# Regrouping the helper copies of the first attention unit, and two rewritten instruction orders, in a block-sparse attention and GELU kernel

## The chip, the cores and the metric

The kernel runs on one core of one Trainium2 chip. The metric is the device time of one execution in microseconds (us), lower is better; it is the time of the single core that is used. A core has TensorE (PE, with weight loads shown apart as PEld), VectorE (DVE), ScalarE (ACT), GpSimd (POOL) and SyncE (SP), each of which works through its own instructions in order, and 16 DMA engines that all queues share.

## The reference

Inputs are q, k and v, each 4 batches x 8 heads x 768 tokens x 64, three sampled block numbers for each of 24 query blocks, and two weight matrices. Attention is block-sparse: a token sees the block of 32 keys that it is in, its two neighbours, the first and the last block, and the sampled blocks; queries of the first and the last block see everything.

```
scores = q @ k^T / 8
mask   = |blk_i - blk_j| <= 1, or blk_i or blk_j is 0 or 23, or blk_j in sampled_blocks[blk_i]
attn   = softmax(where(mask, scores, -1e9))
x      = (attn @ v) as 3072 tokens x 512
out    = gelu_exact(x @ w_in) @ w_out          # w_in 512x2048, w_out 2048x512
```

## The kernel before

Each batch is split in two units, so there are eight. A unit of the first kind (0, 2, 4, 6) holds the query blocks 1 to 11 in three groups of up to four blocks, and the two dense blocks 0 and 23, whose queries see all keys. A unit of the second kind holds the blocks 12 to 22. For each unit the kernel does attention, then the first matrix product with GELU (FFN1, `ffn1_step`), then the second product (FFN2, `ffn2_pieces`), whose 48 matmuls of 128x512 are spread as filler through the attention of the next unit. Unit 0 has no FFN2 before it, so its filler is 32 products whose result nobody reads (`idle_products`); of these, the numbers in the tuple `small` are 32 columns wide and the others 512.

The order of work within an attention is written out by hand, as a string of words that `attention` reads from left to right. A round is one set of scores: in unit 0, rounds 0 to 3 are the dense ones, 4 and 5 are group a, 6 and 7 group b, 8 and 9 group c. For round i, `si` issues the score matmuls (L364), `mi` the row maxima on DVE (L390, L393), `ei` the exponentials on ACT (L407, L411) and `ti` the transposition of the result on DVE (L424, L429). For group g, `wg` multiplies by the values (PE, L489; dense L450), `dg` divides (DVE, L504 to L509) and `og` transposes on PE (L521) and copies to the FFN1's input on ACT (L529; dense L534). `fN` issues N filler products, `G` loads ACT's table for GELU, `S` stores finished outputs, and `x..` runs one of the named extras. Since every engine is in order, a word's place in the string sets what its instructions wait behind. The score banks in PSUM are three, so a score round waits until the exponentials of an earlier round have freed one.

Sampled keys and values are at block numbers known only at run time, so they are gathered into the tile `gb`, one copy for each sampled block (`gather_pairs`, L319): 128x128 for keys, 128x264 for values. In unit 0, DVE copies the keys of group a, POOL those of groups b and c; the values go to `kn` (group a) and `g` (groups b and c), all by POOL but for the three copies of the last block of group c, which ACT makes (extra `xv`). The keys that do not depend on the sampling are called fixed: the neighbours (L295, in three parts called lanes) and the first and last block (L306 by SP's transfers, or L308). DVE makes them for group a (`xj`, `xi`, `xh`), ACT the neighbours for group b (`xf0`, `xf1`) and group c (`xf2`), and SP transfers the first and last block of both groups, six transfers in all.

Four quarters of w_in are asked for on POOL's queue, each between two stretches of gather copies (L161). `later_loads` (`xl`) makes POOL wait for the latest divided tile (L172), then asks for w_out and for the keys and queries of batch 1. After unit 0, DVE copies all its keys into the tile `kv` that unit 1 reads (L789).

Of the kernel before, what the change touches and what calls it, by code (L numbers as in the profile page):

```python
# [20 lines left out]
def kernel(  # L21
# [147 lines left out]

    def hold_loads(x):  # L170

        nc.gpsimd.tensor_copy(mark, x)  # L172
# [108 lines left out]
    def gather_fixed(kT, place, copy=None, part=None, lanes=range(3)):  # L281
# [5 lines left out]
        for run in runs if part != 1 else ():  # L287
            i0 = place[run[0]]
            assert i0 % 3 == 0
            for lane in range(min(3, len(run))):  # L290
                if lane not in lanes:
                    continue
                m, g0 = len(range(lane, len(run), 3)), i0 // 3
                c0, j = BW + KC * lane, run[0] + lane - 1
                copy(  # L295
                    groups[:, g0:g0 + m, c0:c0 + 3 * BW].rearrange("p g (w c) -> p g w c", c=BW)[:, :, :, 0:KC],
                    kT[:, j:j + 3 * m, :].rearrange("p (g w) c -> p g w c", w=3))
# [4 lines left out]
        for to, n0 in ((groups[:, at, 0:3 * KC].rearrange("p g (l c) -> p g l c", c=KC), 0),  # L302
                       (groups[:, at, 4 * BW:GW].rearrange("p g (l x) -> p g l x", x=DW)[:, :, :, NR * BW:DW], NB - 1)):
            if copy is nc.sync:
                for x in range(n):
                    nc.sync.dma_start(out=to[:, x], in_=kT[:, n0:n0 + 1, :].to_broadcast([P, 3, KC]))  # L306
            else:
                copy(to, kT[:, None, n0:n0 + 1, :].to_broadcast([P, n, 3, KC]))  # L308
# [388 lines left out]
    last = block_numbers(grps[2][-1:], ACT)  # L697
# [6 lines left out]
    def fixed(t, *how):  # L704
        gather_fixed(k0, {j: units[0].place[j] for j in grps[t]}, *how)
    fixed(1, nc.sync, 1)
    fixed(2, nc.sync, 1)
# [3 lines left out]
    others |= block_numbers(grps[0], POOL)  # L711
    load_w_in(1)
    gather(units[0], grps[2], others, 0, KC, nc.gpsimd)

    def values_of(t):

        def ask():
            js = grps[t] if t != 2 else grps[t][:-1]
# [25 lines left out]
    attention(units[0], idle_products(32, (30, 31)),  # L744
# [7 lines left out]
               "f2": lambda: fixed(2, nc.scalar.copy, 0), "v0": values_of(0), "v1": values_of(1),  # L752
               "v2": values_of(2), "v": lambda: gather(units[0], grps[2][-1:], last, KC, BW, nc.scalar), "m": more_numbers(J1[3:5]), "n": more_numbers(J1[5:8]),
# [4 lines left out]
    def next_keys(b):  # L758
# [24 lines left out]
    for n, unit in enumerate(units):  # L783
# [3 lines left out]
        if nxt is not None and not fresh:  # L787
            if n == 0:
                nc.vector.tensor_copy(kvs[0][:, :, 0:KC], k0)  # L789
# [79 lines left out]
```

## Time and profile before

| | us |
|---|---|
| median of three runs | 270.31 (269.55 to 270.35) |
| the profiled execution | 270.44 |
| span within it, which the views show | 268.7 |
| PE busy | 248.3 (92% of the span) |
| DVE, ACT, POOL busy | 202.1, 206.8, 110.1 |

Times in the views count from the start of the span. A row of the timeline gives start, duration, engine, source line, operation, output <- inputs with their shapes, and how many instructions stand together; in brackets stands how long the engine was idle before, and what ended that. "issue" is idle time in which the engine waited for nothing that the profile shows. A row of the windows view gives a stretch from:to, its length, then the busy time of PE, PEld, DVE, ACT and POOL with the number of instructions, the granted TensorE clock (1.00 is full speed), the DMA share and GB/s. The first unit's attention lies between about 10 and 37.6, its FFN1 up to 47.5, and the second unit's attention from there to 70.5.

### The profile page before, as it was taken

What the parts mean: (1) busy time and instruction counts of PE and PEld (TensorE: products, weight loads), DVE (VectorE), ACT (ScalarE), POOL (GpSimd) and SP (SyncE); (2) the same over time, 40 slices, a digit from 0 to 9 for tenths busy, and PEclk for the clock granted to TensorE, in tenths of its full rate; (3) what the DMA queues carried; (4) which work ended last, traced back from release to release, by engine and by line L of the source; (5) the groups of instructions that cost most, each with busy time, mean ns of one, the idle gap of its engine ahead of it and who ended that gap; (6) DMA issues with size and microseconds to landing.
All of it is one profiled execution on the core that took longest, in us unless ns stands there. A gap on an engine that the chain in (4) does not pass through costs nothing.

```text
span 268.7 us, 11541 instructions
## 1 busy us (share of the span) xinstructions
PE 248.3 (92%) x4909; PEld 143.5 (53%) x4944; DVE 202.1 (75%) x472; ACT 206.8 (77%) x382; POOL 110.1 (41%) x216
## 2 busy tenths in 40 slices
PE   1799879989999999999999999999999999999994
PEld 1634566455564566545555566455645655465544
DVE  7599878788998987699988986696979891981000
ACT  8789856978869867897879956987799676995611
POOL 7798987854964001934970005900040340000000
PEclk9999999999999999999999999999999999999999
DMA  6999779999999117913995119911101110111012
GB/s 97 186 185 187 110 101 191 205 129 132 99 164 134 44 43 158 118 40 62 136 141 143 43 46 145 91 43 44 40 2 41 44 41 0 41 44 44 0 39 82
DMA packets 76007, 24.42 MB, mean 91 GB/s; under 512 B 65585, under 2 KB 73010, under 8 KB 75954
## 3 DMA queue, kind: packets, MB, share of 16 engines
q0 software_dynamic: 57536, 13.64, 54.6%
q1 hardware_dynamic: 18418, 10.03, 14.5%
q8 instruction: 39, 0.64, 1.0%
q14 instruction: 14, 0.11, 0.1%
HBM read 27.26 MB, written 6.29 MB: 125 GB/s over the span
## 4 chain that ended last, share of the span: by engine, by line
PE 78%; ACT 7%; DVE 5%; issue 4%; DMA 3%; POOL 1%; ACTq 0%; POOLq 0%
PE hp L544 31%; PE op L587 23%; PE av L489 7%; PE sc L364 7%; ACT pp L407 3%; DMA qn<-in_q_dram 3%; PE tx L521 2%; PE op L619 2%; PE pt L241 2%; PE av L450 2%; DVE pT L424 1%; DVE nm L390 1%; PE av L619 1%; ACT pp L411 1%; DVE xh L509 1%
## 5 line engine op out<-in xcount | busy, mean ns | idle before, releaser
L544 PE MATMUL hp<-xT,w_in_sb 128*128 128x384 bf16 (+2 forms) x536 | 84.9, 319 | 0.0
L587 PE MATMUL op<-w_out_sb,g 128*128 128x512 bf16 x302 | 75.5, 380 | 3.5 <-issue 2.5
L407 ACT ACTIVATE pp<-sc,nm 128x256 bf16<-128x256 f32 x176 | 74.0, 543 | 3.7 <-DVE nm L390 3.1
L544 PEld LDWEIGHTS <-w_in_sb 128*128 128x128 bf16 x536 | 51.1, 98 | 32.8
L390 DVE TENSOR_REDUCE nm<-sc 128x4 f32<-128x1024 f32 (+1 forms) x48 | 52.9, 1116 | 12.8 <-PE sc L364 12.8
L566 ACT ACTIVATE g<-hp 128x768 bf16<-128x768 f32 x56 | 45.0, 809 | 22.7 <-PE hp L544 22.6
L587 PEld LDWEIGHTS <-g 128*128 128x128 bf16 x336 | 29.1, 98 | 34.3 <-issue 7.0
L319 DVE COPY gb<-kv 128x392 bf16 x177 | 35.9, 279 | 0.0
L424 DVE STREAM_TRANSPOSE pT<-pp 128x512 f32<-128x512 f32 (+1 forms) x48 | 30.7, 651 | 3.4 <-ACT pp L407 3.4
L319 POOL COPY gb<-kv 128x392 bf16 x54 | 26.4, 535 | 13.7 <-PE av L489 13.4
L172 POOL COPY mark<-gb 1x1 bf16<-1x1 bf16 x6 | 1.1, 179 | 70.9 <-DVE gb L319 70.9
L489 PEld LDWEIGHTS <-pT 64*32 64x32 bf16 (+1 forms) x2400 | 25.2, 91 | 8.9 <-issue 3.9
L489 PE MATMUL av<-kv,pT 64*32 64x130 bf16 (+1 forms) x1344 | 27.5, 221 | 2.4 <-issue 1.8
L529 ACT COPY xT<-tx 128x512 bf16<-128x512 bf16 (+3 forms) x32 | 13.6, 451 | 14.8 <-PE tx L521 14.8
L148 POOL DMA_DIRECT2D kv<-in_v_dram x32 | 23.0, 726 | 2.4 <-issue 2.3
L364 PE MATMUL sc<-gb,qT 64*32 64x256 bf16 x704 | 17.9, 273 | 2.0 <-issue 0.9
L435 ACT ACT_TABLE_LOAD x15 | 19.2, 1283 | 0.3
L509 DVE TENSOR_TENSOR xh<-av,rec 128x512 bf16<-128x512 f32 (+2 forms) x28 | 18.2, 651 | 1.0
L364 PEld LDWEIGHTS <-qT 64*32 64x32 bf16 x832 | 9.9, 90 | 17.1 <-issue 9.0
L393 DVE TENSOR_REDUCE nm<-sc 128x1 f32<-128x768 f32 x16 | 14.8, 943 | 4.5 <-PE sc L364 4.5
L411 ACT ACTIVATE pp<-sc,nm 128x768 bf16<-128x768 f32 x16 | 17.2, 1109 | 1.1 <-DVE nm L393 1.1
L571 ACT COPY os<-op 128x512 f32<-128x512 f32 (+1 forms) x23 | 13.2, 574 | 5.8 <-PE op L619 4.3
(85 smaller groups left out, 257.9 us busy)
## 6 DMA issues: line engine op xcount, KB each, us to landing
out_dram<-os SPq DMA_DIRECT2D x23, 256.0 KB, 2.1
kv<-in_v_dram POOLq DMA_DIRECT2D x32, 96.0 KB, 3.7
w_in_sb<-in_moe_w_in_dram POOLq DMA_DIRECT2D x4, 512.0 KB, 7.8
w_out_sb<-in_moe_w_out_dram POOLq DMA_DIRECT2D x8, 256.0 KB, 8.0
kn<-in_k_dram POOLq DMA_DIRECT2D x4, 384.0 KB, 8.0
qn<-in_q_dram POOLq DMA_DIRECT2D x4, 384.0 KB, 9.1
qn<-in_q_dram POOLq DMA_DIRECT2D x12, 128.0 KB, 5.4
kn<-in_k_dram POOLq DMA_DIRECT2D x12, 128.0 KB, 6.0
```

Of the source, the lines that this page charges most:

```text
L148: nc.gpsimd.dma_start(out=kvs[b % 2][32 * hh:32 * hh + 32, 0:NB, c0:c0 + D], in_=v[b, h].rearrange("(n p) d -> p n d", p=BL))
L319: copy(to[:, None, :], src[:, bass.ds(at[j][r], 1), :])
L364: nc.tensor.matmul(o, lhsT=qT[rows, j // 4, pr, BL * (j % 4):BL * (j % 4) + BL], rhs=rhs(rows, pr), start=True, stop=True)
L390: nc.vector.tensor_reduce(out=nm[:, 0:2 * n].rearrange("p (g j) -> p g j", g=2), in_=A4[:, :, 0:n, :], op=ALU.max, axis=AX.X, negate=True)
L407: nc.scalar.activation(at[:, x // n, x % n], A[:, a:a + 256].rearrange("p (e c k) -> p e c k", e=2, k=BL), AF.Exp, bias=nm[:, x:x + 1])
L411: nc.scalar.activation(pp[:, 0:S].rearrange("p (c k e) -> p c e k", e=2, k=BL), A[:, 0:S].rearrange("p (c e k) -> p c e k", e=2, k=BL), AF ...
L424: nc.vector.transpose(pt.rearrange("p g c x -> p (g c) x")[:, :, 64 * s:64 * (s + n)].bitcast(F32), pp[:, 0:512 * n].bitcast(F32).rearrang ...
L489: nc.tensor.matmul(av[32 * s:32 * (s + w), h, VS * G:VS * G + V2], lhsT=pv[rows, G, c % 4, BL * s:BL * (s + w), c // 4], rhs=src[rows], st ...
L509: nc.vector.tensor_tensor(xh[rows, :, 0:m * D].rearrange("p h (g x d) -> p h g x d", x=2, d=D), a[:, :, :, 0:2 * D].rearrange("p h g (x d) ...
L544: nc.tensor.matmul(hp[:, i, c0:c1], lhsT=w_in_sb[:, ki, (m + i) * P:(m + i + 1) * P], rhs=xTs[n % 2][:, ki, c0:c1], start=(ki == 0), stop= ...
L566: nc.scalar.activation(g[:, m:m + 2, 0:T], hp[:, :, 0:T], AF.Gelu)
L587: nc.tensor.matmul(op, lhsT=g[:, m, t * P:(t + 1) * P], rhs=w_out_sb[:, m, :], start=(m == 0), stop=(m == KOUT - 1))
```

## The change

Six things change, all before the end of unit 1's attention.

1. Group c's fixed keys, three neighbour parts and two blocks, are transferred by SP (`xk`), asked for after the third dense maxima: a transfer of one element of the latest maxima tile goes ahead of them on SP's queue, and waits for it. The ACT copies of these parts are gone. At the start SP has four transfers in place of six, two of them narrower.
2. ACT makes six value copies in place of three at the end of group c (`xv`), now behind the last exponentials; POOL makes three fewer. ACT also copies blocks 0 to 11 of the keys into `kv` (`xy`), and DVE the other 13.
3. The two-block neighbour copy of group b on ACT becomes two copies of one block.
4. The second quarter of w_in is asked for behind the key gathers of group c, the third and the fourth each after nine value copies. `xl` stands before the value copies of ACT.
5. Unit 0's order is another; 22 of its 32 filler products are 32 columns wide, where two were.
6. Unit 1's order is another.

```diff
+    held = const.tile([1, 1], F32, name="held")
+    def hold_transfers(x):
+        nc.sync.dma_start(out=held, in_=x)
...
-                copy(
-                    groups[...][:, :, :, 0:KC],
-                    kT[:, j:j + 3 * m, :].rearrange("p (g w) c -> p g w c", w=3))
+                to = groups[...][:, :, :, 0:KC]
+                if copy is nc.sync:
+                    for x in range(m):
+                        nc.sync.dma_start(out=to[:, x], in_=kT[:, j + 3 * x:j + 3 * x + 3, :])
+                elif copy == nc.scalar.copy:
+                    for x in range(m):
+                        copy(to[:, x], kT[:, j + 3 * x:j + 3 * x + 3, :])
+                else:
+                    copy(to, kT[:, j:j + 3 * m, :].rearrange("p (g w) c -> p g w c", w=3))
...
-                    nc.sync.dma_start(out=to[:, x], in_=kT[:, n0:n0 + 1, :].to_broadcast([P, 3, KC]))
+                    w = min(3, len(js) - 3 * x)
+                    nc.sync.dma_start(out=to[:, x, 0:w], in_=kT[:, n0:n0 + 1, :].to_broadcast([P, w, KC]))
...
-    last = block_numbers(grps[2][-1:], ACT)
+    last = block_numbers(grps[2][-2:], ACT)
...
     fixed(1, nc.sync, 1)
-    fixed(2, nc.sync, 1)
     gather(units[0], grps[1][:2], others, 0, KC, nc.gpsimd)
     load_w_in(0)
     gather(units[0], grps[1][2:], others, 0, KC, nc.gpsimd)
     others |= block_numbers(grps[0], POOL)
+    gather(units[0], grps[2], others, 0, KC, nc.gpsimd)
     load_w_in(1)
-    gather(units[0], grps[2], others, 0, KC, nc.gpsimd)
...
-            first = (4, 2, len(pairs))[t]
+            first = (9, 9, len(pairs))[t]
...
+    def copied_keys(copy, n0, n1):
+        copy(kvs[0][:, n0:n1, 0:KC], k0[:, n0:n1, :])
+    def keys_by_transfer():
+        hold_transfers(st["nm"][0:1, 0:1])
+        fixed(2, nc.sync)
...
-    attention(units[0], idle_products(32, (30, 31)),
-              "xj xp2 xv0 s0 xp3 s1 m0 f1 xv1 f1 e0 xi m1 e1 xh s2 f1 s3 t0 xf0 m2 e2 f1 m3 t1 e3 f2 s4 xf1 f8 m4 "
+    attention(units[0], idle_products(32, (8, 9, 10, ..., 27, 30, 31)),
+              "xp2 xv0 xv1 xp3 s0 xj xi s1 xh m0 s2 m1 e0 e1 xf0 m2 xk t0 s3 m3 f2 t1 s4 e2 s5 xf1 e3 f14 s6 ..."
...
-        1: ("S s0 s1 m0 m1 f8 e0 f4 xk0d t0 f4 e1 s2 f3 xk1 m2 S t1 s3 e2 f3 m3 f2 xq1d xv t2 wa da e3  "
+        1: ("s0 s1 f4 m0 m1 f5 xk0d s3 e0 S f4 s2 m2 t0 e1 xk1 f13 e2 S t1 m3 t2 xq1d e3 wa xq0 xv s5 s4 da m4 "
...
-                nc.vector.tensor_copy(kvs[0][:, :, 0:KC], k0)
+                copied_keys(nc.vector.tensor_copy, NB // 2, NB + 1)
```

On DVE, the head of unit 0 reads as follows before, from the fixed copies of group a (L308, L295) to the maxima of round 5; L393 are the dense maxima m0 to m3, L390 those of rounds 4 and 5, L429 the transpositions t0 to t3.

```order
L308 COPY gb_85<-qT1_87 128x2x3x128
L393 TENSOR_REDUCE nm_496<-sc_461 128x1
L295 COPY gb_85<-qT1_87 128x3x128 x2
L393 TENSOR_REDUCE nm_518<-sc_487 128x1
L295 COPY gb_85<-qT1_87 128x2x3x128
L429 STREAM_TRANSPOSE ptd_90<-pp_514 128x12x32
L393 TENSOR_REDUCE nm_545<-sc_523 128x1
L393 TENSOR_REDUCE nm_550<-sc_533 128x1
L429 STREAM_TRANSPOSE ptd_90<-pp_520 128x12x32
L390 TENSOR_REDUCE nm_583<-sc_557 128x4
L429 STREAM_TRANSPOSE ptd_90<-pp_553 128x12x32
```

The same place in the changed kernel, whose line numbers are shifted (L320 is the old L308, L308 the old L295, L405 the old L393, L402 the old L390, L441 the old L429):

```order
L320 COPY gb_85<-qT1_87 128x2x3x128
L308 COPY gb_85<-qT1_87 128x3x128 x2
L308 COPY gb_85<-qT1_87 128x2x3x128
L405 TENSOR_REDUCE nm_517<-sc_494 128x1
L405 TENSOR_REDUCE nm_528<-sc_507 128x1
L405 TENSOR_REDUCE nm_536<-sc_519 128x1
L441 STREAM_TRANSPOSE ptd_90<-pp_530 128x12x32
L405 TENSOR_REDUCE nm_554<-sc_545 128x1
L441 STREAM_TRANSPOSE ptd_90<-pp_532 128x12x32
L441 STREAM_TRANSPOSE ptd_90<-pp_577 128x12x32
L402 TENSOR_REDUCE nm_632<-sc_560 128x4
```

All three fixed copies now stand ahead of the first maxima, and t2 stands ahead of the maxima of round 4.

On ACT, the end of unit 0's attention before, from the last of the three value copies (L319): the L407 row is round 9's exponentials, the L529 rows copy groups a and b, then c, into FFN1's input, and the L435 rows load the GELU table.

```order
L319 ISA
L319 COPY g<-kv_83 128x264
L407 ACTIVATE pp<-sc,nm 128x2x128 x2
L529 COPY xT_91<-tx 128x4x128 x2
L529 COPY xT_91<-tx 128x2x96 x2
L435 ACT_TABLE_LOAD
L435 ACTIVATE junk<-zero 1x1
```

And in the changed kernel, from round 9's exponentials (L419 is the old L407; L331 the old L319, one of its six pairs of rows; L541 the old L529; L739 is `xy`):

```order
L419 ACTIVATE pp<-sc,nm 128x2x128 x2
L331 ISA
L331 COPY g<-kv_83 128x264
L541 COPY xT_91<-tx 128x4x128
L739 COPY kv_83<-qT_87 128x12x128
L541 COPY xT_91<-tx 128x4x128
L541 COPY xT_91<-tx 128x2x96 x2
L447 ACT_TABLE_LOAD
```

The value copies, six in place of three, moved behind the last exponentials, and `xy` stands between the copies of group a and group b.

More of the change, by code (lines that the diff above doesn't have):

```diff
@@ L743, in more_numbers @@
         return load
-    attention(units[0], idle_products(32, (30, 31)),
[3 rows of a table removed]
+    attention(units[0], idle_products(32, (8, 9, 10, 11, 12, 13, 14, 15, 16, 17, 18, 19, 20, 21, 22, 23, 24, 25, 26, 27, 30, 31)),
+              "xp2 xv0 xv1 xp3 s0 xj xi s1 xh m0 s2 m1 e0 e1 xf0 m2 xk t0 s3 m3 f2 t1 s4 e2 s5 xf1 e3 f14 s6 t2 m4 e4 t3 wd0 m5 wd1 f4 xv2 s7 m6 f2 t4 xm dd f2 e5 f3 m7 e6 t5 f3 od s8 wa t6 e7 m8 da e8 s9 m9 t7 e9 f2 xl xv oa t8 t9 xy wb db wc ob xa xb dc xn Oc G xc",
               {"l": later_loads, "p2": partial(later_pair, 0), "p3": partial(later_pair, 1),
@@ L751 @@
                "f0": lambda: fixed(1, nc.scalar.copy, 0, (1, 2)), "f1": lambda: fixed(1, nc.scalar.copy, 0, (0,)),
-               "f2": lambda: fixed(2, nc.scalar.copy, 0), "v0": values_of(0), "v1": values_of(1),
-               "v2": values_of(2), "v": lambda: gather(units[0], grps[2][-1:], last, KC, BW, nc.scalar), "m": more_numbers(J1[3:5]), "n": more_numbers(J1[5:8]),
+               "k": keys_by_transfer, "y": lambda: copied_keys(nc.scalar.copy, 0, NB // 2), "v0": values_of(0), "v1": values_of(1),
+               "v2": values_of(2), "v": lambda: gather(units[0], grps[2][-2:], last, KC, BW, nc.scalar), "m": more_numbers(J1[3:4]), "n": more_numbers(J1[4:8]),
                "a": lambda: ffn1_ahead(0, (0, 0, P), (0, 1, P)),
```

4 lines of the change are left out of this document (2 added, 2 removed), and 6 rows, old and new, of tables (PLANS, first).

## The prediction

> **What bounds the kernel now.** The windows view, asked for the attention of unit 0 and of unit 1, shows who is full where.
>
> ```profile
> 18.00:22.00 4.00, 4.00 (x71) 1.68 (x71) 3.93 (x6) 3.82 (x6) 2.90 (x12) 1.00 1.33 201
> 22.00:26.00 4.00, 3.96 (x130) 2.22 (x119) 3.69 (x7) 4.00 (x12) 4.00 (x11) 1.00 1.13 176
> 26.00:30.00 4.00, 3.31 (x132) 1.79 (x129) 3.93 (x8) 3.89 (x12) 4.00 (x11) 1.00 0.86 124
> 30.00:34.00 4.00, 2.64 (x127) 1.76 (x128) 3.00 (x7) 3.00 (x8) 3.55 (x11) 1.00 0.62 105
> 47.50:70.50 23.00, 21.61 (x589) 12.35 (x594) 19.64 (x31) 18.88 (x39) 14.83 (x32) 1.00 1.19 141
> ```
>
> Up to 30 us unit 0 is short of ACT: 4.00, then 3.89 of 4 us. PE's load there is partly filler. From 30 us nobody is full, so waits decide. In unit 1, PE has 21.61 of 23.00, so only 1.39 us can be won there at most. ACT's timeline of unit 0 shows the chain from the first exponentials (14.97) to the last copy ahead of the GELU table:
>
> ```profile
> 14.97 2.19 ACT L411 ACTIVATE pp<-sc,nm 128x768 bf16<-128x768 f32 x2
> 17.02 0.91 ACT L295 COPY gb<-qT 128x384 bf16<-128x384 bf16 x2
> 20.11 0.81 ACT L295 COPY gb<-qT 128x768 bf16<-128x768 bf16 x1
> 20.82 1.72 ACT L407 ACTIVATE pp<-sc,nm 128x256 bf16<-128x256 f32 x4
> 22.38 1.33 ACT L295 COPY gb<-qT 128x384 bf16<-128x384 bf16 x3
> 23.60 3.30 ACT L407 ACTIVATE pp<-sc,nm 128x256 bf16<-128x256 f32 x8
> 26.69 0.50 ACT L534 COPY xT<-tx 128x128 bf16<-128x128 bf16 x2
> 27.30 3.44 ACT L407 ACTIVATE pp<-sc,nm 128x256 bf16<-128x256 f32 x8
> 30.58 1.04 ACT L319 COPY g<-kv 128x264 bf16 x3
> 31.83 0.96 ACT L407 ACTIVATE pp<-sc,nm 128x256 bf16<-128x256 f32 x2 [0.21 <-DVE nm L390]
> 32.65 0.57 ACT L529 COPY xT<-tx 128x512 bf16<-128x512 bf16 x1
> 36.14 0.59 ACT L529 COPY xT<-tx 128x512 bf16<-128x512 bf16 x1 [2.92 <-PE tx L521]
> 37.37 0.54 ACT L529 COPY xT<-tx 128x192 bf16<-128x192 bf16 x2 [0.64 <-PE tx L521]
> ```
>
> Round 9's exponentials end at 32.79 and ACT then idles for 2.92 us: group c's values (PE, `wc`) come late. PE's timeline says why. It stops twice in the middle of a row of equal products, with no semaphore to wait for, and POOL's last value copy ends at 33.55, before the second stop does:
>
> ```profile
> 30.70 0.29 PE L364 MATMUL sc<-gb,qT 64*32 64x256 bf16 x4 [0.95 <-issue]
> 34.80 0.29 PE L489 MATMUL av<-kv,pT 64*32 64x130 bf16 x9 [1.18 <-issue]
> 37.63 7.69 PE L544 MATMUL hp<-xT,w_in_sb 128*128 128x128 bf16 x62
> 27.91 5.64 POOL L319 COPY g<-kv 128x264 bf16 x16
> ```
>
> The two stops lie 255 or 256 instructions apart in PE's order. The page has 39 packets of 16 KB on the instruction queue for PE's 9,853 recorded instructions, about 253 for each; the DMA view, asked for three stretches of 0.3 us (from 24.3, 28.3 and 32.4), finds one such packet in each.
>
> ```profile
> PE 248.3 (92%) x4909; PEld 143.5 (53%) x4944; DVE 202.1 (75%) x472; ACT 206.8 (77%) x382; POOL 110.1 (41%) x216
> q8 instruction: 39, 0.64, 1.0%
> q8 instruction: 1, 0.02, 23.3%
> q8 instruction: 1, 0.02, 20.2%
> q8 instruction: 1, 0.02, 21.1%
> ```
>
> I read the stops as PE having run out of instructions: it comes to the end of a block at 29.75, the packet of about 32.5 follows, and the block that it brings is run from 34.80, 5.05 us after. One block in between is already there. So PE cannot enter a block earlier than 5.05 us after it came to the end of the block before the previous one. Going back 2.75 us from the packets near 24.4 and 28.45, the two ends before were reached at 21.7 and 25.7.
>
> **The change, part by part.** *ACT's start.* PE now turns the last query pair ahead of the first dense scores, and DVE makes all fixed copies of group a ahead of the first maxima:
>
> ```profile
> 12.63 0.83 PE L364 MATMUL sc<-qT,qT 64*32 64x512 bf16 x8
> 13.38 0.85 PE L241 MATMUL pq<-identity,qn 96*64 96x96 bf16 x16
> 13.51 0.96 DVE L393 TENSOR_REDUCE nm<-sc 128x1 f32<-128x768 f32 x1 [0.37 <-PE sc L364]
> 14.38 0.60 DVE L295 COPY gb<-qT 128x384 bf16<-128x384 bf16 x2
> 15.92 0.55 DVE L295 COPY gb<-qT 128x768 bf16<-128x768 bf16 x1
> ```
>
> The first scores start at 13.4 instead of 12.63 and end at 14.2; DVE, free from 13.14 (it sat idle 0.37 before 13.51), has made its copies of 0.60 and 0.55 by then. Maxima of 0.96 from 14.25 let the exponentials start at 15.3: +0.3. The other dense maxima follow without a gap, the third ending at 17.1.
>
> *ACT's middle.* Group c's three copies go: 22.38 to 23.60, -1.22. The value copies go from 30.58 to behind round 9: 31.83 - 30.58, -1.25. One copy of two blocks (0.81) becomes two of one, which take 0.91 in the row at 17.02: +0.1. If ACT never idled, round 9 would end 0.3 + 0.1 - 1.22 - 1.25 = 2.07 us earlier, at 30.7. It will idle, I think, in two places. First, the block ends now lie in round 6's scores, reached at 21.2 behind the fourth dense exponentials, and behind round 7's scores, reached at 24.7. PE has to stop there until 21.2 + 5.05 = 26.25; only then come the transposition of the dense output and round 8's scores. ACT's dense copies, in order ahead of round 7's exponentials, would be free at 26.15 and get their input at 26.9: 0.75 idle. Second, round 8's maxima stand on DVE behind round 7's and two transpositions, and round 4's behind t2: about 0.4 together. So round 9 ends at 32.79 - 2.07 + 1.15 = 31.9, 0.9 earlier (bounds 2.07 and 0).
>
> *Group c.* PE comes to the next block end in round 9's scores, which wait for round 7's exponentials (29.1), so the block in `wc` is there at 34.15 instead of 34.80. The six value copies take 2 x 1.04, from 31.9 to 34.0, just in time; POOL has three fewer. Then ACT copies group a (0.57, to 34.5), and `xy`: 1,536 columns, by the step from 384 (0.46 each) to 768 (0.81) 0.81 + 2 x 0.35 = 1.5, to 36.0; bounds 0.9 (DVE's rate, below) and 1.9 (four of 0.46). Only then comes group b's copy, to 36.6; it ended at 36.73 before. Group c's follows, 0.15 to 0.3 earlier than before. So most of the 0.9 is given back to `xy`. DVE's copy shrinks from 1.80 to 13/25 of that, but DVE is late for nobody: PE runs FFN1 until 47.53.
>
> ```profile
> 36.85 1.80 DVE L789 COPY kv<-qT 128x3200 bf16<-128x3200 bf16 x1
> 47.53 0.63 PE L364 MATMUL sc<-gb,qT 64*32 64x256 bf16 x32
> ```
>
> Products of FFN1 that need only groups a and b start about 0.5 earlier, those that need c 0.25. I take -0.4 for the whole of FFN1, since PE fills it. w_in's second to fourth quarters are asked for about 2 us later than before and are first used at 39 us and later: nothing. w_out and the next keys are asked for 2 us earlier, as POOL ends earlier: nothing either, PE has no wait for them in the view.
>
> *SP's transfers.* They are a new wait of round 8's scores.
>
> ```profile
> L306 SPq DMA_DIRECT2D gb<-qT x6: 618/712/2166, 10.4 to 14.2; - x6
> DMA to landing us min/median/max: 7.0/7.4/9.7
> out_dram<-os SPq DMA_DIRECT2D x23, 256.0 KB, 2.1
> ```
>
> The third maxima end at 17.1; six issues of 0.71 put the last one's start at 20.65. Round 8 needs it at 26.9, so it may take 6.2 us. The rows run from 2.1 to 9.7; the 7.0 to 9.7 were measured beside the loads of values, while w_in's second quarter now waits until POOL has made the group's key copies, so I take 5: hidden. The Trainium skill's page "DMA: Bandwidth & Descriptors" (Anatomy of one DMA) puts a transfer at about 2.0 us plus its bytes at 436 GB/s, fitted on GpSimd's path; for 96 KB that would be 2.2 us by estimate, hidden with 4 us to spare, where this trace has 7.0 at the least.
>
> *Unit 1.* The same pieces in another order, on a PE with 1.39 us idle, of which one stop is of the same kind:
>
> ```profile
> 57.43 0.27 PE L489 MATMUL av<-kv,pT 64*32 64x130 bf16 x9 [0.60 <-issue]
> 59.94 0.81 ACT L258 ACTIVATE kv<-pt 128x768 bf16<-128x768 bf16 x1 [0.73 <-PE pt L241]
> ```
>
> Thirteen filler products now stand between the block end and group a's values, so the 0.60 can go. But three fillers that stood between two transpositions sharing a bank are gone, so PE waits for a copy like the one of 0.81 there (about 0.5 after the two score rounds between), and a little for the same reason elsewhere. I take 0, bounds -0.6 and +0.9.
>
> *Sum:* 270.44 - 0.4 + 0 = 270.0 for the profiled execution; the median of the runs is 0.13 below it, so **269.9**.
>
> **The rivals.** *More is won* (0.36): unit 1's stop goes with little in its place (-0.6), and `xy` is as short as 0.9 (a further -0.3): 269.0; if ACT doesn't idle either, about 268.5. For it: ACT really loses 2.5 us of work. Against: the stops of PE.
>
> *The transfers come late* (0.12): the place is round 8's scores. At 7.4 us they land at 28.05, round 8 is 1.1 late, and the gain is gone; this is where it turns. At 9.7 they land at 30.35, 3.4 late; maxima, exponentials, value copies and `xy` all follow, and group c's copies come 2.7 later than in the forecast: 272.6. For it: the rows' own 7.0 to 9.7. Against: fewer of SP's and POOL's packets then.
>
> *Unit 1 gets worse* (0.08): the stop stays and the uncovered copies come on top: 269.9 + 0.9 to 1.4, about 271.1.
>
> *PE's clock falls* (0.04). Twenty fillers of 512 columns, 0.235 each by the next row, become 32 columns wide, 4.7 us less for PE.
>
> ```profile
> 19.08 1.90 PE L600 MATMUL op<-qT,identity 128*128 128x512 bf16 x8
> ```
>
> Half a clock over half a slice of the page (6.7 us) would cost about 3: 273. The row from 30 to 34 us speaks against it: 2.64 of 4.00, clock 1.00. The skill's page "TensorE: Matmul & The Clock Gate" (Part 1) halves the clock after an idle window of about 3.4 us; by that rule it holds, since no idle stretch here comes near, and so far the trace agrees.
>
> **Numbers.** A measurement can tell about 0.3%, 0.8 us, from no change. The forecast (0.40) lies within it. Faster 0.36, slower 0.12 + 0.08 + 0.04 = 0.24, same 0.40. The range reaches from 268.8 (the first rival but for its tail) to 271.4 (unit 1 worse, a transfer of 8 us): about 0.2 is left out. The forecast's own range is 269.5 to 270.7.
>
> **What would show it.** Right: round 9's exponentials end near 31.9; PE has "issue" stops near 26, 30 and 34; the copies of group b stand behind a row of about 1.5 for `xy`; hp starts in full near 37.2; unit 1 lasts 22.5 to 23.9. Wrong: round 8's scores waiting for a DMA; no stop behind round 7's scores; the clock below 1.00; hp in full at 36 or after 38.

## The result, and the profile after

The changed kernel takes 274.03 us (median of four runs, 272.62 to 276.97); the kernel before, beside it, 270.02. The ratio is 1.0132, interval 1.0086 to 1.0179: slower by 1.3% where no change was forecast, and above the range (271.4). The profiled execution took 274.36 with a span of 272.6, 3.9 more than before. This ratio and those below leave out runs that took over 1.5% longer than the fastest of the same kernel.

PE's timeline of the changed kernel shows where the time is lost (the dense output's transposition, the scores of round 9, group c's values, FFN1 in full, unit 1's first scores, FFN1 of unit 1):

```profile
19.56 2.74 PE L612 MATMUL op<-qT,identity 128*128 128x512 bf16 x6
22.56 0.43 PE L376 MATMUL sc<-gb,qT 64*32 64x256 bf16 x16
28.33 0.39 PE L612 MATMUL op<-qT,identity 128*128 128x512 bf16 x1 [2.71 <-issue]
32.81 0.40 PE L376 MATMUL sc<-gb,qT 64*32 64x256 bf16 x4 [1.42 <-issue]
38.55 0.40 PE L501 MATMUL av<-kv,pT 64*32 64x130 bf16 x9 [1.57 <-issue]
42.19 10.41 PE L556 MATMUL hp<-xT,w_in_sb 128*128 128x128 bf16 x76
52.53 0.63 PE L376 MATMUL sc<-gb,qT 64*32 64x256 bf16 x32
74.99 5.20 PE L556 MATMUL hp<-xT,w_in_sb 128*128 128x384 bf16 x31
```

FFN1 starts in full at 42.19 (37.63 before: +4.56), lasts to 52.53 (10.34 in place of 9.90: +0.44), unit 1 lasts 22.46 (22.86: -0.40), and the rest is 0.70 shorter; together +3.9. So the loss lies before 42.19. There PE has three stops without a semaphore, as forecast near 26, 30 and 34, but they end at 28.33, 32.81 and 38.55, after 2.71, 1.42 and 1.57. ACT stands idle after each of them: 2.76, then 1.56 (for the maxima of round 9, whose scores stand behind the second stop), then 2.17.

```profile
15.19 2.08 ACT L423 ACTIVATE pp<-sc,nm 128x768 bf16<-128x768 f32 x2 [0.39 <-DVE nm L405]
20.86 5.25 ACT L419 ACTIVATE pp<-sc,nm 128x256 bf16<-128x256 f32 x12
28.87 0.43 ACT L546 COPY xT<-tx 128x128 bf16<-128x128 bf16 x2 [2.76 <-PE tx L533]
34.05 0.94 ACT L419 ACTIVATE pp<-sc,nm 128x256 bf16<-128x256 f32 x2 [1.56 <-DVE nm L402]
37.18 1.48 ACT L739 COPY kv<-qT 128x1536 bf16<-128x1536 bf16 x1
40.83 0.58 ACT L541 COPY xT<-tx 128x512 bf16<-128x512 bf16 x1 [2.17 <-PE tx L533]
```

And the clock falls. Below are the clock row of the profile's page, and six rows of the windows view for stretches of 3.41 us, whose ends lie where the clock changes or a multiple of 3.41 from there:

```profile
PEclk9998658999999999999999999999999999999999
```

```profile
12.42:15.83 3.41, 3.19 (x49) 1.59 (x45) 3.10 (x8) 2.15 (x3) 2.92 (x8) 1.00 2.23 158
15.83:19.24 3.41, 1.54 (x42) 0.58 (x41) 3.02 (x6) 3.41 (x6) 3.41 (x15) 1.00 1.68 195
19.24:22.64 3.40, 3.40 (x38) 1.09 (x30) 3.21 (x4) 3.30 (x8) 3.40 (x10) 0.50 1.16 183
26.05:29.46 3.41, 1.13 (x74) 0.91 (x75) 2.14 (x4) 0.65 (x4) 3.41 (x10) 1.00 0.87 143
32.87:36.28 3.41, 2.70 (x106) 1.98 (x111) 2.23 (x4) 2.23 (x7) 3.41 (x6) 0.50 0.76 118
39.69:43.10 3.41, 3.41 (x57) 3.08 (x41) 2.30 (x5) 1.24 (x4) 1.70 (x3) 0.50 1.23 205
```

It halves at 19.24, is back at 22.64, halves at 29.46 and is back at 43.10: one, two and four times 3.41 apart. Each fall follows a stretch in which PE was busy 1.54 or 1.13 of 3.41, each rise one in which it was full; 2.70 of 3.41 at half clock brought no rise. The Trainium skill ("TensorE: Matmul & The Clock Gate", Part 1) has a free-running window of 3,413 ns, which agrees. By the same page the clock falls after an idle window; here it also fell after windows in which PE was busy for 33% and 45%, and the measurement decides.

### The profile page after: what moved, and what is told of

It is laid out like the page before. It is cut to its first block, busy times and chain, and to the rows that moved or that the text cites. A ratio compares the mean times of both kernels' runs of the same rounds, so it can differ in the third digit from the quotient of the medians.

```text
span 272.6 us, 11577 instructions
## 1 busy us (share of the span) xinstructions
PE 251.9 (92%) x4944; PEld 146.3 (54%) x4944; DVE 201.4 (74%) x472; ACT 208.0 (76%) x384; POOL 105.6 (39%) x213
## 3 DMA queue, kind: packets, MB, share of 16 engines
q1 hardware_dynamic: 19108, 10.19, 15.0%
## 4 chain that ended last, share of the span: by engine, by line
PE 83%; ACT 7%; issue 3%; DMA 3%; DVE 3%; POOL 1%; POOLq 0%; ACTq 0%
PE hp L556 31%; PE op L599 25%; PE av L501 9%; PE sc L376 6%; DMA qn<-in_q_dram 3%; PE tx L533 2%; PE av L462 2%; PE op L631 2%; ACT pp L419 2%; ACT pp L423 2%; PE pt L246 2%; PE av L631 1%; PE op L612 1%; DVE pT L436 1%; ACT L447 1%
## 5 line engine op out<-in xcount | busy, mean ns | idle before, releaser
L556 PE MATMUL hp<-xT,w_in_sb 128*128 128x384 bf16 (+2 forms) x536 | 85.8, 322 | 0.0
L599 PE MATMUL op<-w_out_sb,g 128*128 128x512 bf16 x336 | 83.1, 380 | 0.3
L419 ACT ACTIVATE pp<-sc,nm 128x256 bf16<-128x256 f32 x176 | 74.0, 543 | 5.4 <-DVE nm L402 5.1
L556 PEld LDWEIGHTS <-w_in_sb 128*128 128x128 bf16 x536 | 52.1, 100 | 32.9
L402 DVE TENSOR_REDUCE nm<-sc 128x4 f32<-128x1024 f32 (+1 forms) x48 | 53.1, 1120 | 17.5 <-PE sc L376 17.4
L331 DVE COPY gb<-kv 128x392 bf16 x177 | 35.3, 279 | 0.1
L501 PEld LDWEIGHTS <-pT 64*32 64x32 bf16 (+1 forms) x2400 | 26.8, 95 | 9.4 <-issue 4.1
L331 POOL COPY gb<-kv 128x392 bf16 x54 | 26.3, 533 | 13.6 <-PE av L501 13.0
L501 PE MATMUL av<-kv,pT 64*32 64x130 bf16 (+1 forms) x1344 | 28.9, 230 | 2.3 <-issue 1.6
L541 ACT COPY xT<-tx 128x512 bf16<-128x512 bf16 (+3 forms) x32 | 13.6, 452 | 14.9 <-PE tx L533 14.9
L376 PEld LDWEIGHTS <-qT 64*32 64x32 bf16 x832 | 10.3, 91 | 17.8 <-issue 11.1
L447 ACT ACT_TABLE_LOAD x15 | 19.2, 1283 | 0.3
L423 ACT ACTIVATE pp<-sc,nm 128x768 bf16<-128x768 f32 x16 | 17.1, 1111 | 0.9 <-DVE nm L405 0.9
L501 PE MATMUL av<-gb,pT 64*32 64x130 bf16 x924 | 17.1, 222 | 0.0
```

Of the source, the lines that this page charges most:

```text
L331: copy(to[:, None, :], src[:, bass.ds(at[j][r], 1), :])
L376: nc.tensor.matmul(o, lhsT=qT[rows, j // 4, pr, BL * (j % 4):BL * (j % 4) + BL], rhs=rhs(rows, pr), start=True, stop=True)
L402: nc.vector.tensor_reduce(out=nm[:, 0:2 * n].rearrange("p (g j) -> p g j", g=2), in_=A4[:, :, 0:n, :], op=ALU.max, axis=AX.X, negate=True)
L419: nc.scalar.activation(at[:, x // n, x % n], A[:, a:a + 256].rearrange("p (e c k) -> p e c k", e=2, k=BL), AF.Exp, bias=nm[:, x:x + 1])
L423: nc.scalar.activation(pp[:, 0:S].rearrange("p (c k e) -> p c e k", e=2, k=BL), A[:, 0:S].rearrange("p (c e k) -> p c e k", e=2, k=BL), AF ...
L447: nc.scalar.activation(junk, zero[0:1, 0:1], func)
```

## The experiments

All timings are ratios to the kernel before, run beside each kernel. The table holds what the comparisons below need: when PE's instruction packets start (DMA view, asked in steps of 0.1 us; the first is at about 14 in all), when FFN1 of unit 0 is in full and how long it takes. The seven rows from after to after_act have w_out and the next keys asked for early, as in the change, the others late.

| run | packets start near | FFN1 full | lasts | ratio, interval |
|---|---|---|---|---|
| before | 24.4, 28.4, 32.5, 36.5 | 37.63 | 9.90 | |
| after | 25.8, 29.6, 36.1, 42.2 | 42.19 | 10.34 | 1.0132, 1.0086 to 1.0179 |
| after_again | 27.9, 33.3, 36.9, 43.8 | 42.55 | 11.24 | 1.0117, 1.0059 to 1.0174 |
| wide | 25.0, 28.8, 33.2, 39.9 | 38.88 | 11.07 | 1.0138, 1.0077 to 1.0200 |
| early | 26.9, 33.2, 39.5, 45.6 | 45.39 | 10.23 | 1.0165, 1.0097 to 1.0233 |
| wide_early | 25.7, 29.6, 35.4, 41.8 | 41.41 | 10.47 | 1.0104, 1.0061 to 1.0147 |
| after_win | 25.8, 32.2, 36.1, 43.6 | 42.86 | 10.89 | 1.0218, 1.0166 to 1.0271 |
| after_act | 24.3, 28.6, 33.6, 41.4 | 38.69 | 12.90 | 1.0079, 1.0045 to 1.0113 |
| late_loads | 26.0, 29.9, 33.7, 37.7 | 39.31 | 9.89 | 1.0019, 0.9989 to 1.0049 |
| wide_late | 26.2, 30.8, 34.7, 38.2 | 40.19 | 9.88 | 1.0026, 0.9998 to 1.0055 |
| late_warm | 26.0, 29.8, 34.0, 37.7 | 39.54 | 9.88 | 1.0070, 1.0039 to 1.0101 |
| act_late | 24.9, 28.6, 33.4, 36.7 | 39.25 | 10.52 | 1.0053, 1.0031 to 1.0075 |
| after_old_loads | 27.1, 31.2, 35.5, 39.0 | 40.86 | 9.89 | 1.0079, 1.0051 to 1.0107 |
| mended | 26.1, 29.7, 33.7, 37.6 | 38.89 | 9.89 | 1.0035, 0.9995 to 1.0075 |
| mended_warm | 25.6, 29.1, 33.2, 36.8 | 38.07 | 9.88 | 1.0007, 0.9985 to 1.0029 |
| mended_act | 24.6, 28.6, 33.7, 37.3 | 38.56 | 10.19 | 1.0048, 1.0027 to 1.0070 |
| mended_win | 26.1, 32.2, 37.7, 41.3 | 42.52 | 9.89 | 1.0116, 1.0071 to 1.0160 |
| before_narrow | 24.5, 30.8, 34.2, 37.7 | 41.35 | 9.90 | 1.0018, 0.9989 to 1.0047 |
| before_cold | 24.5, 31.0, 34.5, 38.0 | 40.44 | 9.89 | 1.0019, 0.9972 to 1.0067 |
| unit1_alone | 24.2, 27.9, 32.3, 36.5 | 37.49 | 9.89 | 0.9989, 0.9971 to 1.0007 |

The times and packets of a row are those of one execution; where a ratio and its row disagree (before_narrow), the ratio, from up to 12 runs, decides. The ratios of wide, early, wide_early and after_win rest on three or four runs each.

**Unit 1.** *unit1_alone*: the kernel before with only the new order of unit 1.

> The kernel before with only the new order of unit 1. Forecast: no change, 269.5 to 270.7. What the trace after suggests: unit 1 lasts 22.46 in place of 22.86, and the rest 197.6 in place of 198.3, so 0.4 to 1.1 faster: 269.0 to 269.7. Rival: unit 1 gained only because unit 0 was late (loads and gathers had more time), and alone it is 0.3 to 0.8 slower: 270.4 to 270.9. Clock 1.00 by all.

No change: 0.9989. The 0.40 that the trace after shows isn't the order's: unit 1 lasted 23.19 here, and with the old order 22.27 in before_narrow and 22.90 in before_cold. Its length varies with how it begins.

**The fillers' width.** *wide*, the changed kernel with wide fillers:

```diff
-    attention(units[0], idle_products(32, (8, 9, 10, ..., 27, 30, 31)),
+    attention(units[0], idle_products(32, (30, 31)),
```

> The changed kernel, with the 20 narrow fillers of 512 columns again (only 30 and 31 stay narrow). Theory (PE's load): the clock falls at 19.2 because PE is busy only 1.54 of the 3.41 us before it, which the wide fillers, all behind that point, cannot mend; so a half clock of one stretch of 3.4 us stays, but the twelve fillers at 24.4 to 25.3 then cover the stop of 2.71, and the second fall at 29.5 is gone. Group c ends some 2 to 3 us sooner than in the changed kernel: 271.0 to 272.5, mean clock 0.99. Rival (order): the new order of unit 0 is late by itself, and the clock only goes with it; then wider fillers win nothing: 273.5 to 275. Rival (fillers in the way): they put back the scores of round 6 by 1.7 us and everything behind: 275 to 276.

The ratio is 1.0138, no better than the changed kernel's, though the clock held at 1.00 in the profiled execution. It rests on three runs that lie far apart: 271.35 and 272.50 at a clock of 1.00, as the theory had it, and 275.19 at 0.994. So this run doesn't settle whether the clock is the loss; before_narrow and late_loads below, where the clock falls and nothing measurable is lost, say more. What the wide fillers do is the rival's: the scores of round 6 start at 24.24 (22.56), and behind ten fillers ACT idles 2.09 for the dense output. *before_narrow* is the reverse, the kernel before with fillers 8 to 27 narrow:

> The kernel before, its order untouched, with the 20 fillers 8 to 27 of 32 columns in place of 512. Theory (PE's load): PE has 3.3 us less work between 18 and 32 us, a stretch of 3.41 us falls under about 1.6 us busy there or behind a block's end, the clock falls, 271.5 to 274, mean clock under 0.99 in most runs. Rival (the clock falls through the new order, not through the width): the clock holds and ACT, no longer held by fillers, gives 269.3 to 270.4.

The clock falls (mean 0.973 to 0.998 over the runs), as that theory said, and yet the ratio is 1.0018. The profiled execution shows a stop of 3.65 at PE's block end and a late FFN1, but over the runs no loss can be told (the interval ends at 1.0047). So narrow fillers make the clock fall, and alone cost too little to measure.

**The fillers' place.** *early* and *wide_early* move six of the fourteen fillers ahead of the scores of round 5, with narrow and with wide fillers behind:

```diff
-... s4 e2 s5 xf1 e3 f14 s6 ...
+... s4 e2 f6 s5 xf1 e3 f8 s6 ...
```

> The changed kernel, narrow fillers as there, but six of the fourteen fillers (the six wide ones) moved from behind the scores of round 5 to ahead of them, where PE idles 1.36 us. Theory (PE's load): the first fall at 19.2 is gone, since PE is then busy about 2.9 of the 3.41 us; the scores of round 6 come 2 us sooner; the stop at a block's end stays, since nothing wide covers it, and so does a fall near 29.5: 271 to 273, mean clock 0.97 to 0.98. Rival (order): no gain from the clock alone, 273.5 to 275. Rival (only the instruction stop matters): the block end is reached 2 us sooner, the stop shrinks from 2.71 to under 1, and the clock holds: 269.5 to 270.5.

> Both edits: wide fillers, and six of them ahead of the scores of round 5. Theory (PE's load): the clock stays at 1.00 in all runs, group c's copies end near 37, the time is 269 to 270.3, that is, what the forecast gave if the clock holds. Rival (order): 272 or more with the clock at 1.00. Rival (fillers in the way): 271 to 272 at clock 1.00, as the wide fillers hold up rounds 6 to 8.

1.0165 and 1.0104. The fall at 19.2 is gone in both, another comes at 28.0 and at 34.3, and nothing is won. Since the clock falls in both, they can't part the clock from the stops. In *early* PE reaches the first block's end sooner, at 22.2, but its packet starts only at 26.9.

**Early loads.** The extra `xl` moves back behind `wc`; *late_loads* does it in the changed kernel, *wide_late* with wide fillers, and *after_again* is the changed kernel once more, on another chip than *late_loads*.

```diff
-... e9 f2 xl xv oa t8 t9 xy wb db wc ob ...
+... e9 f2 xv oa t8 t9 xy wb db wc xl ob ...
```

> The changed kernel with only the extra xl back behind wc, so that w_out and the next keys are asked for after the second divided tile in place of the first. Theory (crowding): the instruction packets of PE wait behind those loads (36.1, 3.3 us after the block before was entered, and 42.2, 3.65 after; 1.7 to 1.8 in the kernel before), so the stop of 1.57 at 38.55 shrinks to under 0.5 and the time falls by 1 to 1.5: 272.4 to 273.2. Rival (the clock alone): the packets come late because PE runs at half clock; no change, 273.5 to 274.8.

> The changed kernel with wide fillers and xl behind wc. Theory (crowding): against the run with wide fillers alone, the stops of 0.50 at 35.75 and 1.03 at 42.22 go, 1 to 1.5 less: 269.8 to 271 where the clock holds. Rival (the clock alone): 271.3 to 272.5 where the clock holds, as with wide fillers alone.

> The changed kernel once more, beside the others on one chip, since the run with late loads was timed on another. Theory (early loads crowd the instruction packets): 272.5 to 274.5, that is 1.5 to 3 us more than late loads alone. Rival (the chip or the hour made that difference): 270.7 to 271.7.

1.0132 and 1.0117 become 1.0019, and 1.0138 becomes 1.0026: of 1.2 to 1.4%, this one word takes 1.0 to 1.1, with narrow and with wide fillers, and without overlap of the intervals. In late_loads the clock still falls, with means of 0.973 to 0.994. With wide fillers the 1.1 hangs on the run of 275.19 at a clock of 0.994: the two runs at a clock of 1.00 are 0.1 and 1.3 us above 271.2, the middle of the six such runs of wide_late. How much of the early loads' cost comes by way of a longer half clock was not taken apart. (Where ACT makes group c's keys, after_act and act_late below, it takes 0.3, with overlapping intervals.) The mechanism stands in the DMA view. Stretches of 0.3 us of the changed kernel, from 36.0 and from 42.1, each with one instruction packet (packets, MB, share of 16 engines):

```profile
q0 software_dynamic: 39, 0.04, 80.0%
q8 instruction: 1, 0.02, 20.3%
...
q0 software_dynamic: 63, 0.06, 125.7%
q8 instruction: 1, 0.02, 20.0%
```

The same with late loads, from 33.6 and from 37.6:

```profile
q8 instruction: 1, 0.02, 28.6%
q0 software_dynamic: 9, 0.01, 12.0%
...
q8 instruction: 1, 0.02, 28.2%
```

POOL asks for w_out at these times in the kernel before, in the changed kernel and with late loads:

```profile
34.47 4.22 POOL L166 DMA_DIRECT2D w_out_sb<-in_moe_w_out_dram  x6
...
32.19 4.22 POOL L166 DMA_DIRECT2D w_out_sb<-in_moe_w_out_dram  x6
...
37.68 4.27 POOL L166 DMA_DIRECT2D w_out_sb<-in_moe_w_out_dram  x6
```

With late loads the packets at 33.7 and 37.7 find the engines all but empty. In the table, the last packet starts 6.1 to 7.8 after the one before it in all seven rows with early loads, and 3.3 to 4.2 after it in all others, the kernel before among them (4.0). That gap could also come from PE reaching its blocks late. So count in PE's order: the traces have a block's start at every 256th instruction, where the stops lie. From PE's entry into the last block of instructions ahead of FFN1 in full (38.55 in the changed kernel, 36.63 with late loads) the last packet starts after 3.7 to 5.4 in the seven rows with early loads and after 1.0 to 1.9 in the thirteen others. In the kernel before it is the next packet that is late: PE enters the following block at 39.58 and the packet starts at 43.5, 3.9 later. That costs nothing, since PE enters that packet's block only at 52.56. The early loads put such a delay onto a packet that PE waits for.

PE meets the delay as stops, late in group c and within FFN1. The profiled execution with wide fillers has 0.50 and 1.03, where FFN1 takes 11.07; without early loads FFN1 takes 9.88 to 9.90 in all rows but two (act_late, where the clock is still halved until 40.5, and mended_act, which I can't explain).

```profile
35.75 0.29 PE L501 MATMUL av<-kv,pT 64*32 64x130 bf16 x9 [0.50 <-issue]
42.22 4.06 PE L556 MATMUL hp<-xT,w_in_sb 128*128 128x384 bf16 x24 [1.03 <-issue]
```

What late_loads keeps is the stop of 2.29 at 28.61, before group c. The next runs ask for its cause.

**SP's transfers and w_in.** *after_win* puts w_in's second to fourth quarters back to the old places, *after_act* makes group c's fixed keys as before:

```diff
...
+    load_w_in(1)
     gather(units[0], grps[2], others, 0, KC, nc.gpsimd)
-    load_w_in(1)
...
-            first = (9, 9, len(pairs))[t]
+            first = (4, 2, len(pairs))[t]
```

```diff
     fixed(1, nc.sync, 1)
+    fixed(2, nc.sync, 1)
...
...
-... m2 xk t0 ... e4 t3 wd0 ...
+... m2 t0 ... e4 t3 xk wd0 ...
...
-               "k": keys_by_transfer, ...
+               "k": lambda: fixed(2, nc.scalar.copy, 0), ...
```

> The changed kernel with w_in's second, third and fourth quarters asked for at the old places. Theory (crowding by w_in): the instruction packet that started at 25.8 and 27.9 starts at 24.4 to 24.5 as in the kernel before, the stop of 2.7 to 4.1 shrinks to 1.5 or less, 271.5 to 273. Rival (SP's transfers or PE's own order hold it): packet at 25.5 or later, 273 to 275. The early w_out and keys still cost what they cost.

> The changed kernel with group c's fixed keys as before: the two blocks by SP at the start, the three neighbour parts by ACT (behind the exponentials of round 4). Theory (crowding by SP's transfers): the packet starts by 24.5, the stop shrinks by 1.5 or more, ACT has 1.2 more work that lies in its idle time before the dense copies: 272 to 273.2. Rival (w_in or PE's own order): packet as in the changed kernel, 273.5 to 275.5.

after_win is the slowest of all, 1.0218; after_act has 1.0079, less than the changed kernel, though the intervals just overlap. PE's timeline of after_win:

```profile
28.30 0.39 PE L612 MATMUL op<-qT,identity 128*128 128x512 bf16 x1 [2.65 <-issue]
...
31.21 0.63 PE L376 MATMUL sc<-gb,qT 64*32 64x256 bf16 x16 [2.36 <-POOL g L331]
```

The same view of after_act:

```profile
26.89 0.39 PE L612 MATMUL op<-qT,identity 128*128 128x512 bf16 x1 [0.23 <-issue]
...
36.02 0.29 PE L501 MATMUL av<-kv,pT 64*32 64x130 bf16 x9 [2.02 <-issue]
...
43.86 2.44 PE L556 MATMUL hp<-xT,w_in_sb 128*128 128x384 bf16 x14 [1.77 <-issue]
```

And of after_again, for the changed kernel:

```profile
30.39 0.59 PE L612 MATMUL op<-qT,identity 128*128 128x512 bf16 x1 [4.12 <-issue]
...
32.07 0.63 PE L376 MATMUL sc<-gb,qT 64*32 64x256 bf16 x16 [0.88 <-DMA gb<-qT]
```

With ACT's copies the first packet comes at 24.3 and the stop near 26 is 0.23; with SP's transfers the packet comes at 25.0 to 27.9 in all twelve rows that have them, and at 24.2 to 24.9 in all others but one (after_old_loads, 27.1, which I can't explain). Three pairs of rows differ only in how group c's fixed keys are made: 25.8 and 24.3 (after, after_act), 26.0 and 24.9 (late_loads, act_late), 25.6 and 24.6 (mended_warm, mended_act, below). I take it from these that the transfers hold up the instruction packet. The evidence is one execution of each kernel, and two executions of the changed kernel lie 2.1 apart. In wide and wide_late the packet is late for another reason too: PE reaches the block's end only at 24.4 and 25.2.

The transfers are late themselves when w_in's quarter is asked for ahead of them. The three neighbour parts in the changed kernel and in after_win (us from asking to landing):

```profile
L303 SPq DMA_DIRECT2D gb<-qT x3: 631/657/702, 17.6 to 19.0; - x3
DMA to landing us min/median/max: 4.6/4.8/4.9
...
L303 SPq DMA_DIRECT2D gb<-qT x3: 632/647/657, 18.1 to 19.5; - x3
DMA to landing us min/median/max: 7.2/7.2/7.2
```

The blocks take up to 9.9 in after_win, and round 8's scores wait for them, to 31.21. (The view names POOL's value copies, which are no input of these scores; the last block was asked for at 21.0, and 9.9 from there is 30.9.) The new place of w_in's quarter, which I took for free, is what the transfers live on. The theory on record for after_win, that w_in crowds out the packet, fails: it starts at 25.8 as before. Undoing several together:

> The changed kernel with group c's fixed keys as before (blocks by SP at the start, neighbours by ACT) and w_out and the next keys behind wc; narrow fillers, both orders, the value copies, the split key copy and w_in's places stay. Theory (both loads crowd out the instruction packets, and the clock only follows): the two gains add up: 269.6 to 270.8, a stop under 0.5 near 26, none over 1 later. Rival (the narrow fillers and PE's order cost by themselves): 271 to 272.5, mean clock under 0.995, as with all loads at their old places.

> The changed kernel with all transfers as before: group c's fixed keys by SP at the start and by ACT, w_in at the old places, w_out and the next keys behind wc. Left are the two orders, the narrow fillers, the six value copies and the split copy of the keys. Theory (the loads are the whole loss): 269.8 to 270.8. Rival (the narrow fillers and the order cost by themselves, through the clock): 271 to 272.5 with a mean clock under 0.99.

*act_late*, ACT's copies and late loads: 1.0053. *after_old_loads*, w_in's places undone as well: 1.0079. The stop near 26 is 0.45 in act_late, but the gains don't add up: its interval overlaps that of late_loads, and ACT has the 1.2 us of copies to do again. The remaining 0.2 to 0.8% of the kernels with late loads I can't assign to one part.

**The clock at the start.** The fillers of the changed kernel at 19.56 take 2.74 for six, under a clock of 0.50. With late loads they take as long where the clock column reads 1.00:

```profile
20.04 2.74 PE L612 MATMUL op<-qT,identity 128*128 128x512 bf16 x6
```

I read this as PE starting at half clock, which the column doesn't show until the first change. By these durations it rises by 18.5 in the kernel before and at 20.7 to 23.9 in most of the changed ones. *late_warm* is late_loads with five fillers earlier (the edit below), *before_cold* the kernel before with its six early ones behind the scores of round 5:

```diff
-... s2 m1 e0 e1 ... s4 e2 s5 xf1 e3 f14 s6 ...
+... s2 m1 f2 e0 e1 ... s4 e2 f3 s5 xf1 e3 f9 s6 ...
```

> The run with late loads (the changed kernel, xl behind wc) with five of the wide fillers moved forward: two ahead of the scores of round 3, three ahead of those of round 5, nine left behind them. Theory (late warm-up): PE starts at half clock, which the clock column does not show, and rises only after a stretch of 3.41 us in which it is nearly full: by 18.5 in the kernel before, at 20.7 to 23.9 in the changed ones. Filled from 12 on, it rises by 19, the scores of round 6 end by 21.7 in place of 23.7, and the time is 1 to 1.5 less than with late loads alone: 269.5 to 270.2. Rival (group c is set by ACT and the block ends, not by the start): no difference, 270.5 to 271.5. Rival (fillers in the way): 271.5 or more.

> The kernel before, with the six fillers that stand between its dense score rounds moved behind the scores of round 5; all fillers as wide as before. Theory (late warm-up): PE idles between the dense rounds, the clock rises at 21 or later in place of 15.5 to 18.5, the dense values and rounds 5 to 7 run at half clock, and the time is 1 to 2 us longer: 271.2 to 272.5. Rival (ACT sets the pace there, PE has slack): 269.8 to 270.7, whatever the clock does before 22.

late_warm rises by about 17 and is no faster than late_loads, 1.0070: the scores of round 6 are done by 21.3, and PE then stands at the block's end for 2.92, since the packet still comes at 26.0. before_cold has 1.0019, but with an interval from 0.9972 to 1.0067, and its ten runs reach from 269.52 to 274.37 with a median of 272.10, against 270.26: that a late rise costs nothing isn't shown by it. What late_warm shows is that an early rise wins nothing where the packet sets the time.

**A version meant to win.** *mended* has wide fillers placed where they hold up little, late loads, and round 9's scores ahead of group a's values; *mended_warm* places twelve of its fillers otherwise: two ahead of the scores of round 3, three ahead of those of round 5, three ahead and four behind those of round 6 (in *mended* six ahead of round 5 and six behind round 6). *mended_act* is mended_warm with group c's keys as before, *mended_win* with w_in's old places. The edit of mended_warm against the changed kernel, from the scores of round 5 on:

```diff
...
-... f14 s6 t2 m4 e4 t3 wd0 m5 wd1 f4 xv2 s7 m6 f2 t4 xm dd f2 e5 f3 m7 e6 t5 f3 od s8 wa ...
+... f3 s6 f4 t2 m4 e4 t3 wd0 m5 wd1 f2 xv2 s7 m6 f2 t4 xm dd e5 m7 e6 od t5 f4 s8 f4 s9 wa ...
```

> The changed kernel with wide fillers, xl behind wc, and the fillers put where they hold up nothing: six ahead of the scores of round 5, six behind those of round 6, two and two around those of round 7, the transposition of the dense output ahead of the next eight, four behind the transposition of group a's last round; the scores of round 9 ahead of group a's values. Theory (load and crowding): the clock holds, ACT idles at most 1 us between 20 and 32, round 9's exponentials end near 32, and the time is 268.8 to 270, under the kernel before. Rival (the regrouped copies are worth nothing): 270 to 271 at clock 1.00. Rival (the clock falls all the same, since ACT needs the time from 31 to 37 in which PE has little): 271 to 273.

> The mended kernel with five fillers put ahead of the scores of rounds 3 and 5 as in the run before this. Theory (late warm-up): the clock rises by 19 in place of 21.7, the first products of FFN1 in full come 1 us sooner than 38.89, the time is 269.3 to 270.2. Rival: no difference to the mended kernel, 270.5 to 271.3.

> The mended kernel with the early fillers, with group c's fixed keys as before. Theory: the stops near 28 and 31 (0.52 and 0.68) and the wait of 0.59 for the transfer go, ACT has 1.2 more to do, of which its idle 1.58 ahead of round 8's exponentials takes most: 269.3 to 270.2. Rival (the transfers cost nothing where PE has wide fillers, and ACT's 1.2 count): 270.5 to 271.5.

> The mended kernel with the early fillers (wide fillers, w_out late), and w_in at the old places. Theory (crowding by w_in): group c's transfers and the packets come sooner, the wait of 0.59 for the transfer and the stops of 0.52, 0.68 and 1.21 shrink together by 1 us or more, and the time is 269.0 to 269.8, under the kernel before. Rival (nothing more to win, PE and the block ends set it): 269.9 to 270.7.

1.0035, 1.0007, 1.0048 and 1.0116. None beats the kernel before; the best equals it. PE's timeline of mended_warm:

```profile
27.26 0.29 PE L376 MATMUL sc<-gb,qT 64*32 64x256 bf16 x4 [0.59 <-DMA gb<-qT]
28.07 0.40 PE L376 MATMUL sc<-gb,qT 64*32 64x256 bf16 x12 [0.52 <-issue]
31.52 1.04 PE L612 MATMUL op<-qT,identity 128*128 128x512 bf16 x4 [0.68 <-issue]
35.70 0.29 PE L501 MATMUL av<-kv,pT 64*32 64x130 bf16 x9 [1.21 <-issue]
38.07 8.17 PE L556 MATMUL hp<-xT,w_in_sb 128*128 128x128 bf16 x65
```

ACT ends round 9's exponentials at 32.35 here (32.79 before), at a clock of 1.00, and still group c's values stop for the block that comes at 35.70, where the kernel before had it at 34.80. And mended_win, forecast to be faster than mended_warm, shows once more that w_in's place guards the transfers: round 8's scores come at 30.44, after 3.59.

## Why the prediction was wrong

*What bounds the kernel.* Right, and not taken far enough. The stops are PE waiting for blocks of instructions. The kernel before has packets at 24.4, 28.4, 32.5 and 36.5, one every 4.0 to 4.1 us: between 24 and 37 it runs at the pace of its instruction supply. The 5.05 from a block's end to the entry of the block after the next isn't a constant: counted by 256 instructions, PE enters blocks at 21.86 and 26.97, where the prediction worked its way back to ends at 21.7 and 25.7, and the next packet starts 2.5, 1.5, 1.8 and 1.7 after the entries at 21.86, 26.97, 30.70 and 34.80. What is nearly the same in all runs is the time from the packet's start to the entry of its block: 2.2 to 2.7 in 49 of 52 stops. No run had the last of them before 36.5 or FFN1 in full before 37.49, whatever ACT was relieved of. That this chain is why the 2.5 us of ACT's work bring nothing is argued from these rows; no run took the supply itself away.

*The step that failed.* "w_out and the next keys are asked for 2 us earlier, as POOL ends earlier: nothing either, PE has no wait for them in the view." PE has none for their data; its instructions come through the same engines. The last packet ahead of FFN1 then starts 3.7 after PE enters the block before it, in place of 1.7. FFN1 in full came at 42.19, where the forecast had 37.2; with late loads it came at 39.31. Taken back in the changed kernel, it is worth 1.0 to 1.1 points of the 1.2 to 1.3. The reason given was wrong as well: POOL ends its copies at 31.16 in the changed kernel and at 31.68 with late loads, where it asks for w_out only at 37.68, so it is the new place of `xl` that makes the request early. I had priced moved loads by who waits for their data, though I had just read the stops as late packets.

*PE's stop until 26.25.* Too short: 28.33. Two terms failed. The scores of round 6 were reached at 22.56, not 21.2, since the fillers ran at half clock (2.74 for six in place of 1.4). And the packet started at 25.8, held up, as I read it, by SP's transfers; even where those scores are done at 21.3 (late_warm) it comes no earlier than 26.0. ACT idled 2.76 where I had 0.75, and round 9's exponentials ended at 34.99, not 31.9.

*SP's transfers.* Their own landing was nearly right: 4.8 and 7.0 against 5, the last issue ending at 21.08, hidden in the profiled execution. In after_again the slowest took 11.1 and round 8's scores waited 0.88: the rival with its turn at 7.4 does occur. What I had not thought of is what they do to the packets. w_in's places, "nothing", are worth 0.9 to 1.1 points beside these transfers (1.0132 and 1.0218, whose intervals just overlap; 1.0007 and 1.0116 in mended_warm and mended_win).

*The clock.* The rival with 0.04 happened in every run of the changed kernel (mean 0.967 to 0.993), and its 273 is near the result, for another reason: the clock falls as well in late_loads and before_narrow, at 1.0019 and 1.0018. The rows I set against it (2.64 of 4.00 busy, clock 1.00) were those of before; I had not worked out how much busy time a stretch of 3.41 keeps after the change. The rival's size was luck too: it priced 6.7 us of half clock, and the profiled execution had 17.0 (19.24 to 22.64 and 29.46 to 43.10).

*The small terms.* First exponentials 15.19 (15.3), third maxima 16.88 (17.1), `xy` 1.48 (1.5), unit 1 without effect: right.

## What to carry to other kernels

Count instruction supply as a resource: where PE stops in the middle of equal products with no semaphore, see how far apart its instruction packets start, and ask of each transfer that is moved which packets it will stand in front of, not only who waits for its data. Work taken from an engine brought nothing here while such a chain set the pace. One profiled execution can be several us from the median where the clock falls in some runs: let the ratio decide, and undo one part at a time on the changed kernel.

## What was unexpected of the hardware

- The last instruction packet (16 KB) ahead of FFN1 starts 3.3 to 4.2 us after the one before it in the thirteen rows without early loads, and 6.1 to 7.8 in the seven where the loads of w_out (256 KB each) and of the next keys and queries (384 KB) fill the DMA engines; counted from PE's entry into the last block ahead of FFN1 in full, 1.0 to 1.9 and 3.7 to 5.4.
- The clock changes on a grid of 3.41 us. It halved after stretches with PE busy 1.54 and 1.13 of 3.41; at half clock, 2.70 of 3.41 (32.87 to 36.28) didn't bring it back, and full ones did.
- The clock column reads 1.00 until the first change although the durations are those of half clock: 2.74 for six products of 512 columns in late_loads, against 1.90 for eight at full clock in the kernel before.
